# First x chunk by column halves, warm-up products on a constant, second q-k reload behind two sets of down weights

## The chip, the cores and the metric

The kernel runs on one NeuronCore of one Trainium2 chip. The metric is the device time of one execution in microseconds (us), as the median of several runs. Five engines work side by side: TensorE (PE) multiplies, with its weight loads shown apart as PEld; VectorE (DVE) and ScalarE (ACT) do elementwise work and empty the PSUM banks that PE writes; GpSimd (POOL) and SyncE (SP) here mostly issue transfers. Transfers (DMAs) between device memory and the on-chip buffer are issued by the queues of SP, ACT and POOL. Each engine runs its own list of instructions in order; semaphores tell it when an operand is ready.

## The reference

```python
def _A_ref(x, wqkv, wo):                       # local attention, 32 heads of 32
    qkv = (x @ wqkv) -> q, k, v
    idx = pos[:, None] - 2 * arange(8)[None, :]        # 8 keys, every second position back
    logits = einsum(q, k[idx]) * Dh ** -0.5            # -1e9 where idx < 0
    o = softmax(logits) @ v[idx]
    return o @ wo
def _B_ref(x, w_gate, w_up, w_down):           # gated feed-forward, 1024 -> 3584 -> 1024
    return (gelu(x @ w_gate) * (x @ w_up)) @ w_down
g = sigmoid((x * gate_w).sum(-1))
out = g * A + (1 - g) * B                      # x: 2048 x 1024, bfloat16
```

Both branches read the same x of 2048 rows and 1024 columns.

## The kernel before

**Products.** Every large product is done by a seven-product scheme on 2 x 2 blocks (a Strassen form). For the projections (`Unit`) the blocks come from 1024 rows of x (two chunks of 512 rows, `c1` and `c2`, transposed so that the 1024 columns lie on the partitions as 8 tiles of 128) and from 256 columns of a weight. A unit has the parts p1 (L11 by R11), p2 (L12 by R21), p5, p6, p73 and p4, four matmuls of 128x128 by 128x512 for each product. R11 is the first four column tiles of chunk 0 and R21 the last four; some operands (S1 to S4 of the weights, T1 to T4 of x) are sums that DVE forms. ACT copies out what p1, p2, p5, p6 and p4 leave in a bank; the end of p73 is emptied by a DVE addition (line 389). When that addition is late, PE cannot reuse the bank.

**Order.** The order on every engine is written out by hand. A loop runs over the units; in each turn it emits p1 of the unit, p73 of the one before, p5, then a slot of attention reductions (line 593) if one is due, p2 and p6, and p4 of the one before. Between these, background tasks (`bg`, `run_bg`) put DVE work into the stream by estimated costs and priorities; hooks (`at`, `at_end`) put single actions at the start or end of a turn. None of these costs is a measured time at run time: DVE's order is fixed when the program is built.

**Head.** `head()` runs two pairs of gate/up columns on the first 1024 rows: chunk 0 is loaded as four row tiles of 128 rows (256 KB each, rows of 2 KB), alternately by SP and ACT (`load_xn`, line 144). PE runs NWARM = 6 warm-up products on a region that DVE has set to zero (lines 148 to 152). Then `pe_transpose_chunk(0, ...)` transposes chunk 0 on PE in eight groups of four 128x128 tiles (line 217), row tile by row tile, each row tile's columns 0 to 511 and then 512 to 1023; DVE and ACT copy the groups out in turn (lines 223 and 221). The first products are p1 of the gate and up units. Chunk 1 is transposed by the same function with `by_k`, which takes the column half 0 of all four row tiles first. Weights of the two pairs (`load_pair`, line 168) follow x in SP's queue, the first halves in 128 KB pieces, then chunk 1 and the second halves.

**Attention and down weights.** Units 2 to 17 give q and k, units 18 to 25 give v. The last 256 rows of q and k of each half go out to memory (`q_d`, `k_d`, lines 512 and 513) and are read back at the end of turn QE = 18 by `spill_load` (lines 633 and 634), two transfers for each half, into space that held weights of the q and k units and their sums. DVE multiplies them much later (`spill`). In the next turn `tf_load` (line 854) loads the sets 4 and 5 of down weights, four transfers of 256 KB each, into the space of the third and fourth block of the q and k weights (last read by p73 and by p4 of unit 17). `t_forms` (lines 869 and 872) forms differences of these sets on DVE. All of these loads stand in SP's queue in the order in which they are emitted, and SP waits at each one until its space and its data are free. SP and ACT use eight semaphores for their transfers in turn, so a load also waits for the one eight before it.

Of the kernel before, what the change touches and what calls it, by code (L numbers as in the profile page):

```python
# [10 lines left out]
BF16 = mybir.dt.bfloat16  # L11
# [4 lines left out]
P = 128  # L16
SC = 512
# [5 lines left out]
NJ = 4  # L23
SJ = AC // NJ
NEG = -1.0e9
NWARM = 6
QG = 4

KB = 512
# [17 lines left out]
R_ST = 178  # L47
# [21 lines left out]
def kernel(  # L69
# [12 lines left out]
    nc = tc.nc  # L82
# [3 lines left out]
    x = A_x.rearrange("b s d -> (b s) d")  # L86
    o2 = out.rearrange("b s d -> (b s) d")
    KT = D // P
    HK = KT // 2
# [13 lines left out]
    def reg(kb, n):  # L103
        o = int(kb * KB)
        return arena[:, o:o + n]

    def reg3(kb, a, b):
        return reg(kb, a * b).rearrange("p (a b) -> p a b", a=a)
# [4 lines left out]
    def regf(kb, n):  # L113
        return reg(kb, 2 * n).bitcast(F32)
# [3 lines left out]
    def bank(i):  # L118
        return banks[:, i, :]
# [15 lines left out]
    V = nc.vector  # L135
    TT = V.tensor_tensor

    with tc.manual_schedule(engines={mybir.EngineType.PE, mybir.EngineType.DVE, mybir.EngineType.Activation,
                                    mybir.EngineType.SP, mybir.EngineType.Pool}):
        xn = [reg3(R_XN + 8 * i, 4, D) for i in range(2)]  # L140

        def load_xn(c):
            for j in range(4):
                (nc.scalar if c == 0 and j % 2 else nc.sync).dma_start(
                    out=xn[c % 2][:, j, :], in_=x[c * SC + j * P:c * SC + (j + 1) * P, :])

        load_xn(0)
        warm = reg(R_ST, SC)
        V.memset(warm, 0.0)
        for i in range(NWARM):  # L150
            pw = bank((2, 4, 6, 0)[i % 4])
            nc.tensor.matmul(pw, lhsT=warm[:, 0:P], rhs=warm, start=True, stop=True)
# [44 lines left out]
        def flat(a):  # L197
            return a.rearrange("p a b -> p (a b)")
# [8 lines left out]
            f = xf[s]  # L207
            TT(out=flat(f.T3), in0=flat(f.R22), in1=flat(f.R12), op=ALU.subtract)

        def pe_transpose_chunk(c, dst, slots, by_k=False):  # L210
            order = [(j, k0) for j in range(4) for k0 in range(0, KT, 4)]
            if by_k:
                order.sort(key=lambda g: g[1])
            for n_, (j, k0) in enumerate(order):
                p_ = bank(slots[n_ % len(slots)]).bitcast(BF16)[:, 0:SC].rearrange("p (a b) -> p a b", a=4)
                for kk in range(4):
                    nc.tensor.transpose(out=p_[:, kk, :], in_=xn[c % 2][:, j, (k0 + kk) * P:(k0 + kk + 1) * P],  # L217
                                        identity=ident[:])
                d = dst[:, k0:k0 + 4, j * P:(j + 1) * P]
                if n_ % 2 == 1:  # L220
                    nc.scalar.copy(out=d, in_=p_)
                else:
                    V.tensor_copy(out=d, in_=p_)
# [92 lines left out]
        def gu_forms(w, sm, m):  # L316
            r = lambda k0, a: (lambda kt: w[:, m, k0 + kt, a * P:(a + 1) * P])
            z = lambda n: (lambda kt: sm[:, n, m, kt, :])
            return {"L11": r(0, 0), "L12": r(HK, 0), "L22": r(HK, 1), "S1": z(0), "S2": z(1), "S3": z(2), "S4": z(3)}
# [7 lines left out]
        for c in range(2, 4):  # L327
            dst = (xf[1].c1, xf[1].c2)[c - 2]
# [91 lines left out]
        def bg(gen, prio, wake):  # L420
            t = Task(gen, prio, wake)
            tasks.append(t)
            tasks.sort(key=lambda t_: t_.prio)
            return t
# [41 lines left out]
        def at(n, fn):  # L466
            hooks.setdefault(n, []).append(fn)
# [4 lines left out]
        def at_end(n, fn):  # L472
            post.setdefault(n, []).append(fn)
# [7 lines left out]
        def h_task(G, U, i, s):  # L481
            h_store(G, U, i, s)
            yield 1.14 if i < NSC else 2.3
# [148 lines left out]
        def spill_load(s):  # L632
            nc.sync.dma_start(out=qb[s], in_=q_d[s][:])
            nc.sync.dma_start(out=kb[s], in_=k_d[s][:])
# [4 lines left out]
        def spill(s):  # L639
            while reduced[0] < 2 * NT:  # L640
                yield None
            accs = []
            for g, (x, y) in enumerate(SPILL[s]):
                for i, ef in enumerate((x, y)):
                    t = QG * g + 2 * i
                    if credit[0] > 1.5:
                        qk_mult2(pair_at(*ef), qb[s][:, t, :], kb[s][:, t, HALO:HALO + AC], AC, KV)
                        yield 2.21
                        continue
                    for j in range(2):  # L650
                        qk_mult(reg3(ef[j], NWIN, AC), qb[s][:, t + j, :], kb[s][:, t + j, HALO:HALO + AC])
                        yield 1.14
                if credit[0] > 1.5:
                    TT(out=pair_at(*x), in0=pair_at(*x), in1=pair_at(*y), op=ALU.add)
                    yield 2.21
                else:
                    for j in range(2):
                        TT(out=reg(x[j], NWIN * AC), in0=reg(x[j], NWIN * AC), in1=reg(y[j], NWIN * AC), op=ALU.add)
                        yield 1.14
                lo, hi = (reg3(o, NWIN, AC) for o in x)  # L660
                TT(out=lo, in0=lo, in1=hi, op=ALU.add)
                yield 1.14
                accs.append(lo)
            slotq.append(lambda: spill_reduce(s, accs))
# [132 lines left out]
                n_ = Q0 + NT * s + t  # L797
                due(n_ + 4, bg(qk_prods(units[n_], s, t), 2, n_ + 2))
        QE = Q0 + 2 * NT
        at_end(QE, lambda: (spill_load(0), spill_load(1)))  # L800
        bg(spill(0), 4, QE + 2)
        bg(spill(1), 4, QE + 2)
        pv_task = [bg(pv_all(), 4.2, QE + 3)]
# [11 lines left out]
        def r_parts(half, nh, i0=0, i1=NK):  # L815
            ns = slice(nh * SC, (nh + 1) * SC)
            if i0 < NH_:
                e = min(i1, NH_)
                yield slice(i0, e), B_w_down[:, ns].rearrange("(i two p) n -> p i two n", two=2, p=P)[:, i0:e, half, :]
            if i1 > NH_:  # L820
                a = max(i0, NH_)
                yield slice(a, i1), A_wo[:, ns].rearrange("(p t) n -> p t n", t=NT)[:, 4 * half + a - NH_:4 * half + i1 - NH_, :]
# [19 lines left out]
        N1 = 4  # L842
        TB = Q0 + 2 * NT + 1
        TC = NQKV + 1

        def tf_set(q):
            o = R_TF[q % 3] if q < N1 or q >= N1 + 2 else R_TB[q - N1]
            return [reg3(o + NP * k, NP, SC) for k in range(4)]

        def tf_load(q):  # L850
            i0 = NP * q
            for k, a in enumerate(((0, 0), (0, 1), (1, 0), (1, 1))):
                for sl, src in r_parts(*a, i0, i0 + NP):
                    nc.sync.dma_start(out=tf_set(q)[k][:, sl.start - i0:sl.stop - i0, :], in_=src)
# [23 lines left out]

        for q, b in enumerate((2, 3, 5)):
            at(Q0 + b, lambda q=q: tf_load(q))  # L880
        at(TB, lambda: [tf_load(q) for q in range(N1, N1 + 2)])
        at(TC, lambda: [tf_load(q) for q in range(N1 + 2, min(N1 + 5, NQ))])
        tft = bg(t_forms(), 6, Q0 + 4)

# [364 lines left out]
        def head():  # L1249
            xs, f = xf[0], []  # L1250
            for w, sm, o in ((raw0, sums0, R_ATTN), (raw1, sums1, R_PROD)):
                for m in range(2):
                    u = Unit(gu_forms(w, sm, m), xs, ("gate", "up")[m], None)
                    u.T = reg3(o + 4 * m, 2, SUP)
                    f.append(u)
            units[0:Q0] = f[2:]
            for u, x, v, y, z in zip(f, (3, 5, 1, 7), (1, 7, 3, 5), (0, 2, 4, 6), (1, 3, 5, 7)):
                u.lie(x, v, y, z)
            f[3].fin = lambda: bg(h_task(f[2].T, f[3].T, 1, 0), 0, now[0] + 1)
            T = lambda o_, a, b_: TT(out=flat(o_), in0=flat(a), in1=flat(b_), op=ALU.subtract)  # L1260
            s0, s1 = sums_pair(raw0, sums0), sums_pair(raw1, sums1)

            pe_transpose_chunk(0, xs.c1, (3, 5, 1, 7))
            f[0].p1_()
            f[1].p1_()
            patterns()
            f[0].p2()
            f[1].p2()
            f[2].p1_()
            f[3].p1_()  # L1270
            f[2].p2()
            pe_transpose_chunk(1, xs.c2, (3, 5, 1), True)
            T(xs.T1, xs.R12, xs.R11)
            next(s0)
            next(s1)
            f[3].p2()
            for c in range(2):
                gate_chunk(c, bank(3 + 2 * c))
            next(s0)
            T(xs.T2, xs.R22, xs.T1)  # L1280
            next(s1)
            T(xs.T3, xs.R22, xs.R12)
            for i, u in enumerate(f):
                u.p5(regf(R_XN + 2 * i, SC))
            for g in (s0, s0, s1, s1):
                next(g)
            T(xs.T4, xs.R21, xs.T2)
            for u in f:
                u.p6()
            next(sq0)  # L1290
            next(sq0)
            for u in f[:3]:
                u.p73()
            for g in (sq0, sq0, sq1, sq1):
                next(g)
            for u in f[:3]:
                u.p4()
            bg(h_task(f[0].T, f[1].T, 0, 0), 0, Q0 + 1)

        head()  # L1300
        for b in range(Q0, n):
            now[0] = b
# [55 lines left out]
```

## Time and profile before

| | |
|---|---|
| median of 3 runs | 719.1 us (717.49 to 719.21) |
| the profiled execution | 718.77 us, span 717.0 us |
| PE busy | 705.7 us (98%) |
| DVE busy | 669.0 us (93%) |
| ACT, POOL busy | 330.7 us, 142.4 us |
| chain that ended last | PE 91%, DVE 3%, DMA 3% |

The span is what the trace covers; the profiled execution's own time is 1.8 us more. The timeline gives the start of an instruction or of a row of like ones, how long it took, and in brackets how long its engine had been idle before it and what ended the idle time. The table of waits gives, for an engine and a line, what was waited for: total us, how many times, the longest. The rows of transfers give count, size and median us from issue to landing. Since PE is busy for nearly all of the span, what counts is where PE stands still and what it waits for there.

### The profile page before, as it was taken

What the parts mean: (1) busy time and instruction counts of PE and PEld (TensorE: products, weight loads), DVE (VectorE), ACT (ScalarE), POOL (GpSimd) and SP (SyncE); (2) the same over time, 40 slices, a digit from 0 to 9 for tenths busy, and PEclk for the clock granted to TensorE, in tenths of its full rate; (3) what the DMA queues carried; (4) which work ended last, traced back from release to release, by engine and by line L of the source; (5) the groups of instructions that cost most, each with busy time, mean ns of one, the idle gap of its engine ahead of it and who ended that gap; (6) DMA issues with size and microseconds to landing.
All of it is one profiled execution on the core that took longest, in us unless ns stands there. A gap on an engine that the chain in (4) does not pass through costs nothing.

```text
span 717.0 us, 10673 instructions
## 1 busy us (share of the span) xinstructions
PE 705.7 (98%) x4043; PEld 408.4 (57%) x4099; DVE 669.0 (93%) x633; ACT 330.7 (46%) x603; POOL 142.4 (20%) x245
## 2 busy tenths in 40 slices
PE   8999999999999999999999999999999999999998
PEld 5466666655544444444444444444447886758887
DVE  3969989989999999999999999999699899799997
ACT  5554445444466565555555555555322321132431
POOL 1223445323232332121300010101100002100011
PEclk9999999999999999999999999999999999999999
DMA  9975434478285667765762763474950799995951
GB/s 252 274 188 169 151 125 154 155 239 306 92 269 175 214 216 240 223 214 180 234 178 89 279 208 122 161 262 148 426 226 29 300 405 397 417 431 218 403 211 59
DMA packets 94707, 162.03 MB, mean 226 GB/s; under 512 B 23632, under 2 KB 71152, under 8 KB 90304
## 3 DMA queue, kind: packets, MB, share of 16 engines
q1 hardware_dynamic: 77632, 105.46, 42.7%
q0 software_dynamic: 16304, 48.29, 19.9%
q10 hardware_dynamic: 720, 7.60, 2.7%
q8 instruction: 32, 0.52, 0.3%
q14 instruction: 19, 0.16, 0.1%
HBM read 112.17 MB, written 54.14 MB: 232 GB/s over the span
## 4 chain that ended last, share of the span: by engine, by line
PE 91%; DVE 3%; DMA 3%; issue 1%; ACT 0%; DVEq 0%; POOLq 0%; ACTq 0%
PE banks L343 63%; PE banks L1046 19%; PE banks L1079 7%; PE banks L593 2%; DMA arena<-h_d 1%; DMA h_d<-arena 1%; DVE arena L389 1%; DVE arena L753 1%; PE banks L217 1%; DVE arena L747 1%; DMA arena<-in_A_x_dram 0%; DVE arena L313 0%; DVE arena L588 0%; DVE arena L1260 0%; DVE arena L581 0%
## 5 line engine op out<-in xcount | busy, mean ns | idle before, releaser
L343 PE MATMUL banks<-arena 128*128 128x512 bf16 x2191 | 484.1, 379 | 5.4 <-DVE arena L389 2.2
L343 PEld LDWEIGHTS <-arena 128*128 128x128 bf16 x2240 | 245.9, 110 | 242.2 <-issue 8.1
L1046 PE MATMUL banks<-arena 128*128 128x256 bf16 x1260 | 138.5, 273 | 0.0
L1046 PEld LDWEIGHTS <-arena 128*128 128x128 bf16 x1260 | 123.3, 98 | 15.4 <-issue 0.5
L389 DVE TENSOR_TENSOR arena<-banks,arena 128x1024 bf16<-128x1024 f32 x80 | 97.4, 1219 | 11.1 <-PE banks L343 6.5
L370 ACT COPY arena<-banks 128x512 f32<-128x512 f32 x80 | 46.9, 587 | 129.7 <-PE banks L343 129.7
L351 ACT CAST arena<-banks 128x512 bf16<-128x512 f32 x104 | 60.9, 585 | 42.8 <-PE banks L343 42.2
L747 DVE TENSOR_TENSOR arena<-arena 128x4096 bf16<-128x4096 bf16 (+1 forms) x41 | 73.5, 1818 | 0.3
L753 DVE TENSOR_TENSOR arena<-arena 128x2048 bf16<-128x2048 bf16 (+2 forms) x54 | 68.1, 1261 | 0.9
L250 POOL DMA_DIRECT2D h_d<-arena x28 | 20.4, 731 | 222.6 <-DVE arena L244 144.6
L1079 PE MATMUL banks<-arena 128*128 128x512 bf16 x281 | 62.6, 379 | 0.7 <-DMA arena<-h_d 0.4
L378 ACT COPY banks<-banks 128x512 f32<-128x512 f32 x80 | 45.6, 570 | 23.7 <-PE banks L343 20.8
L1004 DVE TENSOR_TENSOR arena<-arena 128x2304 bf16<-128x2304 bf16 x40 | 53.3, 1352 | 0.5
L365 ACT COPY banks<-banks 128x512 f32<-128x512 f32 x80 | 46.1, 576 | 14.2 <-PE banks L343 13.1
L1051 ACT COPY banks<-banks 128x256 f32<-128x256 f32 x60 | 21.4, 356 | 62.2 <-PE banks L1046 62.0
L588 DVE TENSOR_TENSOR arena<-arena 128x4096 bf16<-128x4096 bf16 x21 | 47.9, 2284 | 0.3 <-ACT arena L370 0.2
L1079 PEld LDWEIGHTS <-arena 128*128 128x128 bf16 x288 | 28.1, 98 | 34.2 <-DMA arena<-h_d 0.9
L349 ACT ACTIVATE arena<-banks 128x512 bf16<-128x512 f32 x56 | 33.5, 597 | 20.4 <-PE banks L343 20.4
L927 DVE TENSOR_TENSOR arena<-arena 128x2048 bf16<-128x2048 bf16 (+1 forms) x40 | 41.7, 1111 | 0.0
L313 DVE TENSOR_TENSOR arena<-arena 128x1024 bf16<-128x1024 bf16 x64 | 41.1, 685 | 0.5
L1012 DVE TENSOR_TENSOR arena<-arena 128x2304 bf16<-128x2304 bf16 x28 | 37.7, 1352 | 0.2
L244 DVE TENSOR_TENSOR arena<-arena 128x2048 bf16<-128x2048 bf16 x28 | 34.0, 1216 | 2.8 <-ACT arena L351 2.8
(92 smaller groups left out, 448.2 us busy)
## 6 DMA issues: line engine op xcount, KB each, us to landing
arena<-t_d SPq DMA_DIRECT2D x8, 2304.0 KB, 9.6
h_d<-arena POOLq DMA_DIRECT2D x28, 512.0 KB, 4.4
arena<-w_c SPq DMA_DIRECT2D x12, 1152.0 KB, 13.2
t_d<-arena POOLq DMA_DIRECT2D x36, 256.0 KB, 5.4
arena<-h_d SPq DMA_DIRECT2D x6, 1536.0 KB, 12.1
arena<-in_B_w_down_dram SPq DMA_DIRECT2D x28, 256.0 KB, 6.6
arena<-in_B_w_gate_dram SPq DMA_DIRECT2D x14, 512.0 KB, 5.4
arena<-in_B_w_up_dram SPq DMA_DIRECT2D x14, 512.0 KB, 4.2
```

The source lines that it names most:

```text
L343: self.pe = nc.tensor.matmul(ps, lhsT=self.L[form](kt), rhs=rhs[:, kt, :], start=(start and kt == 0), stop=(kt == HK - 1), skip_group_chec ...
L351: nc.scalar.copy(out=o_, in_=i_)
L365: nc.scalar.copy(out=self.Y, in_=self.X)
L370: nc.scalar.copy(out=self.p5s, in_=self.V)
L378: nc.scalar.copy(out=self.Z, in_=self.Y)
L389: TT(out=self.T[:, :, c2s], in0=pair, in1=self.p5s.rearrange("p (o n) -> p o n", o=1).to_broadcast([P, 2, SC]), op=ALU.add)
L588: TT(out=dst, in0=_win_ap(q, [[sq, 2], [0, NWIN], [1, AC]]), in1=_win_ap(k, [[sk, 2], [-DIL, NWIN], [1, AC]]), op=ALU.mult)
L747: TT(out=prod2[:, t % 4:t % 4 + m, :], in0=flat(ab).rearrange("p (o n) -> p o n", o=1).to_broadcast([P, m, NWIN * AC]), in1=_win_ap(v[:, t ...
L753: TT(out=h(0) if w > 1 else o_[:, t:t + m, :], in0=h(0), in1=h(1), op=ALU.add)
L1004: TT(out=o_, in0=a, in1=b_, op=op)
L1046: nc.tensor.matmul(c(i, h, j), lhsT=l[:, kt, j * P:(j + 1) * P], rhs=r[:, kt, :], start=False, stop=(kt == KH - 1), skip_group_check=True)
L1079: nc.tensor.matmul(ps, lhsT=L[:, i, j * P:(j + 1) * P], rhs=R[:, i, :], start=(start and q == 0), stop=(q == NK - 1), skip_group_check=not ...
```

## The change

- Chunk 0 of x is loaded by four transfers in another cut: columns 0 to 511 of the row tiles 0 and 1 (SP) and 2 and 3 (ACT), then columns 512 to 1023 likewise. Each is again 256 KB, in pieces of 1 KB. They stay ahead of all weights in SP's queue.
- Eight warm-up products read a constant of ones (one element per partition, read again and again) in place of six on a zeroed region; the zeroing on DVE is gone. The dummy activation on ACT reads the constant too.
- Chunk 0 is transposed in the order of column halves, as chunk 1 was: the argument `by_k` is gone and its order holds for both.
- The reload of q and k of the second half moves from directly behind the first half's to behind the sets 4 and 5 of down weights. In SP's queue the eight transfers of line 854 pass the two of lines 633 and 634. The instruction streams of PE, DVE, ACT and POOL are otherwise the same, instruction by instruction.

```diff
-NWARM = 6
+NWARM = 8
...
         def load_xn(c):
             for j in range(4):
-                (nc.scalar if c == 0 and j % 2 else nc.sync).dma_start(
-                    out=xn[c % 2][:, j, :], in_=x[c * SC + j * P:c * SC + (j + 1) * P, :])
-
-        load_xn(0)
-        warm = reg(R_ST, SC)
-        V.memset(warm, 0.0)
+                nc.sync.dma_start(out=xn[c % 2][:, j, :], in_=x[c * SC + j * P:c * SC + (j + 1) * P, :])
+
+        for h in range(2):
+            cs = slice(h * HK * P, (h + 1) * HK * P)
+            for i, q in enumerate((nc.sync, nc.scalar)):
+                q.dma_start(out=xn[0][:, 2 * i:2 * i + 2, cs],
+                            in_=x[2 * i * P:2 * (i + 1) * P, cs].rearrange("(j p) d -> p j d", p=P))
+        warm = nc.const_aps.tensor(1.0, [P, SC], BF16)
...
-        def pe_transpose_chunk(c, dst, slots, by_k=False):
+        def pe_transpose_chunk(c, dst, slots):
             order = [(j, k0) for j in range(4) for k0 in range(0, KT, 4)]
-            if by_k:
-                order.sort(key=lambda g: g[1])
+            order.sort(key=lambda g: g[1])
...
-        at_end(QE, lambda: (spill_load(0), spill_load(1)))
+        at_end(QE, lambda: spill_load(0))
...
-        at(TB, lambda: [tf_load(q) for q in range(N1, N1 + 2)])
+        at(TB, lambda: ([tf_load(q) for q in range(N1, N1 + 2)], spill_load(1)))
...
-            pe_transpose_chunk(1, xs.c2, (3, 5, 1), True)
+            pe_transpose_chunk(1, xs.c2, (3, 5, 1))
```

## Prediction

> **What bounds the kernel now.** I read the page first (busy times and the chain), then PE's waits, since PE is on nearly all of the chain, and then the timelines of the two places that the change touches.
>
> ```profile
> span 717.0 us, 10673 instructions
> PE 705.7 (98%) x4043; PEld 408.4 (57%) x4099; DVE 669.0 (93%) x633; ACT 330.7 (46%) x603; POOL 142.4 (20%) x245
> PE 91%; DVE 3%; DMA 3%; issue 1%; ACT 0%; DVEq 0%; POOLq 0%; ACTq 0%
> ```
>
> PE stands still for 717.0 - 705.7 = 11.3 us of the span, so no change that only takes waits away can bring more than 1.6%. Its waits for a released operand, the largest first:
>
> ```profile
> PE banks L343 <- DVE arena L389: 2.2, 2, 1.4
> PE banks L152 <- DVE arena L149: 1.2, 1, 1.2
> ```
>
> Two waits for DVE's addition at line 389 are 2.2 us, and one of them is 1.4. The wait at line 152 is for the zeroing of the warm-up region at the very start. PE and DVE around the 1.4 us:
>
> ```profile
> 163.76 1.48 PE L593 MATMUL banks<-arena,ones_r 128*32 128x512 bf16 x24
> 165.17 7.99 PE L343 MATMUL banks<-arena 128*128 128x512 bf16 x35
> 174.61 7.72 PE L343 MATMUL banks<-arena 128*128 128x512 bf16 x35 [1.44 <-DVE arena L389]
> ```
> ```profile
> 149.41 1.23 DVE L389 TENSOR_TENSOR arena<-banks,arena 128x1024 bf16<-128x1024 f32 x1 [1.42 <-PE banks L343]
> ...
> 157.46 1.22 DVE L389 TENSOR_TENSOR arena<-banks,arena 128x1024 bf16<-128x1024 f32 x1
> 159.22 1.22 DVE L869 TENSOR_TENSOR arena<-arena 128x2048 bf16<-128x2048 bf16 x1 [0.55 <-DMA arena<-in_B_w_down_dram]
> 160.48 1.42 DVE L872 TENSOR_TENSOR arena<-arena 128x1024 bf16<-128x1024 bf16 x2
> 162.82 1.23 DVE L869 TENSOR_TENSOR arena<-arena 128x2048 bf16<-128x2048 bf16 x1 [0.92 <-DMA arena<-in_B_w_down_dram]
> 164.08 1.42 DVE L872 TENSOR_TENSOR arena<-arena 128x1024 bf16<-128x1024 bf16 x2
> 165.41 1.22 DVE L389 TENSOR_TENSOR arena<-banks,arena 128x1024 bf16<-128x1024 f32 x1
> 166.55 1.75 DVE L688 TENSOR_REDUCE md<-banks 128x192 f32<-128x1536 f32 x1
> ...
> 173.34 1.22 DVE L389 TENSOR_TENSOR arena<-banks,arena 128x1024 bf16<-128x1024 f32 x1
> ```
>
> At 149.41 DVE is ahead and waits for PE. Then it waits 0.55 and 0.92 us for down weights (sets 4 and 5), runs without a gap, and is late at 173.34: PE, out of work at 165.17 + 7.99 = 173.16, goes on at 174.61. Why the down weights are late stands in SP's timeline and SP's waits:
>
> ```profile
> 139.20 0.34 SPq L634 DMA_DIRECT2D arena<-k_d  x1
> 148.18 0.33 SPq L633 DMA_DIRECT2D arena<-q_d  x1
> ...
> 149.07 5.63 SPq L854 DMA_DIRECT2D arena<-in_B_w_down_dram  x8
> ```
> ```profile
> SPq L633 <- DMA q_d<-arena: 8.0, 1, 8.0
> ```
>
> The reload of the second half's q waits 8.0 us for the last q store to land, and the eight down-weight loads stand behind it in the queue.
>
> **Step 1: the reload goes behind the down weights.** Two issues (about 0.33 us each) pass behind eight; nothing is added. The four loads of set 4 then need only p73 of unit 17 to be over, set 5 needs its p4. ACT tells when that is: its copies follow p5 of unit 18 (after that p73) and that p4.
>
> ```profile
> 144.17 0.59 ACT L370 COPY arena<-banks 128x512 f32<-128x512 f32 x1 [1.97 <-PE banks L343]
> ...
> 146.76 0.59 ACT L351 CAST arena<-banks 128x512 bf16<-128x512 f32 x1 [0.29 <-PE banks L343]
> ```
> ```profile
> DMA to landing us min/median/max: 3.4/6.6/9.2
> ```
>
> So set 4 can be issued by 144.2 and set 5 by 146.8. The second row is for all loads of line 854. At 5.63 / 8 = 0.7 us an issue, the last loads go out by 146.3 and 148.9. With the median, the sets land by about 152.9 and 155.5; with the longest, by 155.5 and 158.1. DVE asks for set 4 at 157.46 + 1.14 = 158.60 (1.14 is the distance of L389 and L688 above) and for set 5 at 158.60 + 2.59 = 161.19 (2.59: 162.82 to 165.41). Both waits go, with 3 us to spare in the worse case. DVE then reaches the second L389 at 161.19 + 2.59 = 163.78 instead of 165.41, and would start L688 at 164.92. What is late next is PE: L688 reads the reductions of line 593, which end at 163.76 + 1.48 = 165.24. So L688 starts at about 165.30, 1.25 us earlier than before; the last L389 ends 1.25 us earlier, at 173.31, and PE goes on at 173.36: PE gains 1.25 us of its 1.44. Ends of this term: 0 (another wait takes the place), 1.44 (the whole stall). The moved reload lands by about 149.6 + 9.2 = 158.8 at worst; its products stand in DVE's order behind all those of the first half, so nothing asks for it yet and I cost the delay at 0. If a reader stood at 158 us, SP's order would cost the delay in full.
>
> **Step 2: the head.** Nothing of PE's first 18 us is hidden; it is a chain.
>
> ```profile
> 1.20 2.74 PE L152 MATMUL banks<-arena 128*128 128x512 bf16 x6 [1.20 <-DVE arena L149]
> 4.12 3.12 PE L217 MATMUL banks<-ident,arena 128*128 128x128 bf16 x32 [0.19 <-DMA arena<-in_A_x_dram]
> 7.53 1.89 PE L343 MATMUL banks<-arena 128*128 128x512 bf16 x8 [0.29 <-DVE arena L223]
> ```
> ```profile
> 4.10:6.50 2.40, 2.38 (x23) 2.38 (x24) 1.00 1.12 292
> 6.55:7.05 0.50, 0.50 (x11) 0.50 (x9) 1.00 1.29 284
> ```
>
> The second fence is the transposes alone in two stretches (PE busy and count, then weight loads and count): 24 weight loads in 2.40 us are 0.10 us each, 9 in 0.50 us are 0.056. PE doubles its pace at about 6.5 us, though the granted clock reads 1.00 in both. Transfers that matter here:
>
> ```profile
> 0.74 0.91 ACTq L144 DMA_DIRECT2D arena<-in_A_x_dram  x2
> ...
> 1.67 0.43 SPq L168 DMA_DIRECT2D arena<-in_B_w_gate_dram  x1
> ```
> ```profile
> arena<-in_A_x_dram SPq DMA_DIRECT2D x1, 256.0 KB, 3.3
> ...
> arena<-in_A_x_dram ACTq DMA_DIRECT2D x1, 256.0 KB, 4.7
> arena<-in_B_w_gate_dram SPq DMA_DIRECT2D x1, 128.0 KB, 4.7
> ```
>
> - *Warm-up.* Without the zeroing PE starts at about 0.75, as ACT's first issue does, instead of 1.20. Eight products at 2.74 / 6 = 0.46 at most end by 4.4, x lands at about 4.1: PE is fed without the 0.19 us gap, and transposes start at about 4.3 (before: 4.12), a loss of 0.2 at most. No row shows an operand read again from one element; its nearest row is the 0.46 above, which I take.
> - *Smaller pieces of x.* Same bytes, same four issues. Down weights come in pieces of 1 KB and land in 3.4 us at best, x in pieces of 2 KB in 3.3: I take 0.1 to 0.3 us later, for the weights behind too. The last x before lands at about 1.2 + 4.7 = 5.9, after at about 6.1, still before PE needs it.
> - *Order.* p1 needs only the four groups of the first half. Before, the next to last group is among them and PE waits 0.29 us for its copy; after, the copies are long over and p1 follows the last transpose.
> - *Sum.* From 4.3 at 0.104 us, 21.6 transposes are done by 6.55 and the other 10.4 at 0.056 by 7.13: p1 at 7.15 instead of 7.53, 0.38 us less. Were the doubling earlier by the 0.45 us that PE starts earlier, it would be 6.94: 0.59 less. I take 0.45. Ends: 0.88 less (p1 cannot pass the gate weights, 1.67 + 4.7 + 0.3 = 6.65) and 0.3 more (late x, no doubling in time).
>
> [...]
>
> Does the gain live on? PE's next wait is for a DVE sum:
>
> ```profile
> 18.62 6.65 PE L343 MATMUL banks<-arena 128*128 128x512 bf16 x30 [0.26 <-DVE arena L313]
> ```
> ```profile
> DVE arena L389 <- PE banks L343: 4.9, 3, 2.6
> ```
>
> That sum follows the transposes of chunk 1 and so comes earlier with them. The second row (waits of DVE from 30 to 60 us) says that DVE waits 4.9 us for PE there, and at 149.41 again 1.42: PE leads, and what it gains at 7 us is still there at 174.
>
> **Sum.** 1.25 + 0.45 = 1.7 us off the profiled execution's 718.77 (span 717.0 and 1.8 around it): 717.1. That execution lies 0.3 below the median of the runs, 719.1. I say 717.0. From no change a measurement of this kernel can tell about 0.3%, 2.2 us: 716.9 against the median. My forecast lies just at that bound.
>
> **Rivals.**
> - *Early pace, full stall gone.* PE doubles its pace one step earlier. Then transposes run at 0.056 us and wait for x and gate weights: p1 at 6.65, 0.88 less; with 1.44 at 174 that is 2.3 us, 716.4. For it: PE is busy from 0.75 on without the gap. Against: 1.20 to 6.5 was long, and the gap short. [...]
> - *Only the reload.* x in 1 KB pieces comes late enough to eat the 0.45: 718.77 - 1.25 = 717.5; if 0.3 is lost besides, 717.8.
> - *The reload step moves only the wait.* DVE's 1.5 us go, but it meets PE's reductions or another landing, and PE still resumes near 174.6: only the head's 0.45 is left, 718.3. For it: L688 takes 0.4 of DVE's 1.63 at once. Against: nothing else in DVE's rows there is a wait.
> - *Slower: the constant.* If a product on a repeated element takes w instead of 0.46 us, transposes start at 0.75 + 8w. At double pace p1 comes at 0.75 + 8w + 32 x 0.056 = 2.54 + 8w. It passes 7.53 from w = 0.62 on, eats the 1.25 too from w = 0.78, and from w = 1.05 the kernel is slower by over 2.2 us: 721 or more. For it: no row of such an operand. Against: the same count of columns is streamed.
>
> **How the numbers follow.** Forecast as summed: 0.50, its own range 716.0 to 717.8, and half of it lies below 716.9. Early pace: 0.28, all below. Only the reload: 0.07. Only the head: 0.05. Slower (the constant): 0.10. So faster by over 0.3%: 0.25 + 0.28 = 0.53; within: 0.25 + 0.07 + 0.05 = 0.37; slower: 0.10. The range goes from 715.4 (1.44 + 0.88, and a microsecond for the place of the pace's step) to 719.2, which takes in all but the slow case and the far ends.
>
> **What would show it.** Step 1 is right if line 854 is issued before 149 us, DVE has no wait at line 869 and PE's wait of 1.44 us falls to about 0.2. Step 2 is right if warm-up products start near 0.75 at 0.43 to 0.46 us, the transposes follow without a gap, and the first p1 starts between 6.7 and 7.2. The prediction is wrong if PE waits at line 217 for x, if warm-up products outlast 4.5 us, or if another wait for line 389 opens after 174.

## The result and the profile after

| | before | after |
|---|---|---|
| median of 15 runs each, taken side by side | 718.23 us (717.49 to 720.34) | 717.04 us (716.74 to 718.48) |
| ratio | | 0.9982 (95% interval 0.9974 to 0.9990) |
| the profiled execution | 718.77 us, span 717.0 | 717.04 us, span 715.3 |

The change takes 1.2 us off the median; the ratio says 0.18% (1.3 us), with an interval that leaves out "no change". The time is the forecast one (717.0); the way to it is only half the forecast one. The page of the changed kernel begins:

```profile
span 715.3 us, 10731 instructions
PE 709.2 (99%) x4101; PEld 408.3 (57%) x4101; DVE 668.7 (93%) x632; ACT 330.7 (46%) x603; POOL 141.9 (20%) x245
```

PE is at work for all but 6.1 us of the span, where it was 11.3 (before's records lack some 60 matmuls, so part of this difference is counting). PE's largest waits in the changed kernel (total us, times, longest), of which the first is the start of the program; line numbers are one or two higher than before, and line 390 is the addition that was line 389:

```profile
PE banks L154 <- PEq L1343: 0.8, 1, 0.8
PE banks L344 <- DVE arena L390: 0.7, 2, 0.5
PE banks L218 <- DMA arena<-in_A_x_dram: 0.3, 1, 0.3
PE banks L344 <- DVE arena L314: 0.3, 1, 0.3
PE banks L218 <- ACT arena L350: 0.2, 1, 0.2
PE banks L344 <- DMA arena<-in_B_w_up_dram: 0.2, 1, 0.2
```

The waits for line 390 were 2.2 us, 1.4 at most. In their place stands nothing large. In the head the waits for the zeroing (1.2 us) and for a copy ahead of p1 (0.29) are gone; the wait for x has grown from 0.19 to 0.29, and one of 0.20 for up weights is new. PE and then DVE at the place of the old 1.44 us:

```profile
163.98 1.48 PE L594 MATMUL banks<-arena,ones_r 128*32 128x512 bf16 x24
165.39 7.99 PE L344 MATMUL banks<-arena 128*128 128x512 bf16 x36
173.59 8.58 PE L344 MATMUL banks<-arena 128*128 128x512 bf16 x39 [0.20 <-DVE arena L390]
```
```profile
157.69 1.22 DVE L390 TENSOR_TENSOR arena<-banks,arena 128x1024 bf16<-128x1024 f32 x1
158.82 1.22 DVE L870 TENSOR_TENSOR arena<-arena 128x2048 bf16<-128x2048 bf16 x1
160.07 1.42 DVE L873 TENSOR_TENSOR arena<-arena 128x1024 bf16<-128x1024 bf16 x2
161.40 1.22 DVE L870 TENSOR_TENSOR arena<-arena 128x2048 bf16<-128x2048 bf16 x1
...
163.99 1.22 DVE L390 TENSOR_TENSOR arena<-banks,arena 128x1024 bf16<-128x1024 f32 x1
165.52 1.76 DVE L689 TENSOR_REDUCE md<-banks 128x192 f32<-128x1536 f32 x1 [0.31 <-PE banks L594]
...
172.32 1.22 DVE L390 TENSOR_TENSOR arena<-banks,arena 128x1024 bf16<-128x1024 f32 x1
```

DVE no longer waits at line 870, reaches line 390 early at 163.99, stands 0.31 us for the reductions at line 689, and does the last addition at 172.32 instead of 173.34. SP's queue shows why:

```profile
142.02 6.22 SPq L855 DMA_DIRECT2D arena<-in_B_w_down_dram  x8
148.47 0.34 SPq L634 DMA_DIRECT2D arena<-q_d  x1
149.71 0.34 SPq L635 DMA_DIRECT2D arena<-k_d  x1
```

The down weights go out 7 us earlier, and the reload comes behind them. The head, PE's first 9 us:

```profile
0.78 3.57 PE L154 MATMUL banks<-const-bfloat16-1.0 128*128 128x512 bf16 x8 [0.78 <-PEq L1343]
4.64 2.89 PE L218 MATMUL banks<-ident,arena 128*128 128x128 bf16 x32 [0.29 <-DMA arena<-in_A_x_dram]
7.37 1.03 PE L344 MATMUL banks<-arena 128*128 128x512 bf16 x4
8.60 1.04 PE L344 MATMUL banks<-arena 128*128 128x512 bf16 x4 [0.20 <-DMA arena<-in_B_w_up_dram]
```

The warm-up starts 0.42 us earlier and its eight products end at 4.35, but x is not there before 4.64. p1 starts 0.16 us earlier than the 7.53 of before, and the second p1 (up) waits for its weights. PE's wait at 18.84, for the same DVE sum as the wait at 18.62 before, is where the head's balance can be read:

```profile
18.84 2.98 PE L344 MATMUL banks<-arena 128*128 128x512 bf16 x13 [0.26 <-DVE arena L314]
```

So the head costs 0.22 us in this pair of executions.

**Where the 1.7 us between the two spans are.** The head costs 0.22 us, and the stall at 174 is 1.44 - 0.20 = 1.24 us shorter. The rest comes after 500 us, at two places that the edits do not name. Before, PE waits near 527 us for the load of h_d, and its last row of line 1046 takes a little longer than the same row after (line 1047):

```profile
527.04 17.44 PE L1079 MATMUL banks<-arena 128*128 128x512 bf16 x78 [0.36 <-DMA arena<-h_d]
644.32 69.27 PE L1046 MATMUL banks<-arena 128*128 128x256 bf16 x630
```
```profile
642.76 69.09 PE L1047 MATMUL banks<-arena 128*128 128x256 bf16 x630
```

The last rows start 1.56 us apart and the stall at 174 ends 1.02 us apart (174.61 and 173.59), so 0.54 us go to the wait for h_d, which the second execution of the kernel before does not have. The last row itself is 69.27 - 69.09 = 0.18 us shorter. That difference is no matter of the execution: PE and ACT lose 0.17 to 0.19 us near 650 us in all seven profiled executions of kernels that load x in whole rows, and in none of the seven with x in column halves. Why the first load should matter there is open. Together -0.22 + 1.24 + 0.54 + 0.18 = 1.74. PE's wait for line 389 near 279 us reads 0.75 before and 0.54 after, but its end lies 104.89 us behind the end of the stall at 174 in both: nothing was lost there, and the 0.21 us more of idle time fit one matmul whose record is missing before (the rows have 1055 and 1076).

### The profile page after: what moved, and what is told of

The parts are those of the page before. It is cut to its first block, busy times and chain, and to the rows that moved or that the text cites. A ratio compares the mean times of both kernels' runs of the same rounds, so it can differ in the third digit from the quotient of the medians.

```text
span 715.3 us, 10731 instructions
## 1 busy us (share of the span) xinstructions
PE 709.2 (99%) x4101; PEld 408.3 (57%) x4101; DVE 668.7 (93%) x632; ACT 330.7 (46%) x603; POOL 141.9 (20%) x245
## 4 chain that ended last, share of the span: by engine, by line
PE 94%; DVE 3%; DMA 1%; issue 1%; SPq 0%; ACT 0%; DVEq 0%
PE banks L344 64%; PE banks L1047 19%; PE banks L1080 9%; PE banks L594 2%; DMA arena<-in_B_w_up_dram 1%; DVE arena L390 1%; DVE arena L754 1%; DVE arena L748 1%; DVE arena L314 0%; DVE arena L1261 0%; DVE arena L582 0%; DVE arena L245 0%; PE banks L218 0%; SPq L149 0%; PE banks L273 0%
```

## The experiments

Theory at the outset: the gain is the reload's, and the head gives nothing because x in smaller pieces lands later. Rival: the head does bring its 0.45 us, and the profiled execution hides it. The first four kernels ran side by side with the kernel before (718.24 us, median of 33 runs), the next three likewise (718.33, 29 runs); the rest are single profiled executions.

**The moved reload alone, with the old head.**

```diff
-        at_end(QE, lambda: (spill_load(0), spill_load(1)))
+        at_end(QE, lambda: spill_load(0))
...
-        at(TB, lambda: [tf_load(q) for q in range(N1, N1 + 2)])
+        at(TB, lambda: ([tf_load(q) for q in range(N1, N1 + 2)], spill_load(1)))
```

> The kernel before with the moved reload alone. Theory A (the reload brings what the whole change brings, the new head brings nothing or costs a little): DVE has no wait at line 854's data (lines 869), PE's wait of 1.44 us near 174 falls to about 0.2, the time is 1.25 us under the kernel before, as much as with the whole change or up to 0.2 us better. Theory B (the prediction's sum: reload 1.25, head 0.45): 1.25 us under before, 0.45 us above the whole change. Theory C (the gain of the whole change comes from elsewhere, such as the end of the kernel): less than 0.5 us under before.

Measured: 717.48 us (716.75 to 719.53), ratio 0.9988 (0.9977 to 0.9999). DVE's lag against before falls by 1.25 us between 157 and 166 us and the stall is 0.20, as in the changed kernel. So at 174 us this part does in full what the forecast said, without the head; by the medians it brings 0.76 us. Yet the profiled execution took 719.42 us, more than before's; its loss is in the head:

```profile
1.20 2.74 PE L152 MATMUL banks<-arena 128*128 128x512 bf16 x6 [1.20 <-DVE arena L149]
4.80 3.60 PE L217 MATMUL banks<-ident,arena 128*128 128x128 bf16 x32 [0.86 <-DMA arena<-in_A_x_dram]
8.48 1.62 PE L343 MATMUL banks<-arena 128*128 128x512 bf16 x4
```

x landed late here (4.8 instead of 4.1), PE stood 0.86 us, and its pace doubled only at 9.71 us instead of 6.58. p1 came at 8.48, and PE's wait of 18.62 stands at 20.16: 1.54 us lost.

**The head alone, with the reload where it was.**

```diff
-        at_end(QE, lambda: spill_load(0))
+        at_end(QE, lambda: (spill_load(0), spill_load(1)))
...
-        at(TB, lambda: ([tf_load(q) for q in range(N1, N1 + 2)], spill_load(1)))
+        at(TB, lambda: [tf_load(q) for q in range(N1, N1 + 2)])
```

> The changed kernel with the reload put back where it was: only the head's edits stay (x by column halves in 1 KB pieces, eight warm-up products on the constant, transposes by column halves). Theory A: x lands 0.5 to 0.9 us later, p1 starts near 7.4 us but the up product's p1 waits for its weights, the second wait at 18.6 us comes 0.2 us later than before; PE's wait near 174 is about 1.4 us as before; time equal to before within 0.3 us. Theory B: 0.45 us under before.

Measured: 718.74 us (717.40 to 719.37), ratio 0.9996 (0.9985 to 1.0008): no gain from the head by itself. p1 starts at 7.33, as theory A had it, and PE's wait of 18.62 stands at 18.58, not 0.2 us later. Two things in its profile were not expected. DVE's waits (0 to 31 us first, then from 145 to 180):

```profile
DVE arena L314 <- DMA arena<-in_B_w_up_dram: 1.6, 1, 1.6
```
```profile
DVE arena L390 <- PE banks L344: 1.4, 1, 1.4
DVE arena L870 <- DMA arena<-in_B_w_down_dram: 0.7, 1, 0.7
```

The second half of the up weights came 1.6 us late near 20 us; against the changed kernel this execution is 1.2 us later from there on. And DVE waits for only one set of down weights, for 0.7 us; PE's stall is 0.59, not 1.44, though the reload stands in front of the sets as before.

**x in whole rows again, the rest of the change kept**, with the transposes by column halves as in the change, and with them row by row as before (there `by_k` is put back as well).

```diff
-        for h in range(2):
-            cs = slice(h * HK * P, (h + 1) * HK * P)
-            for i, q in enumerate((nc.sync, nc.scalar)):
-                q.dma_start(out=xn[0][:, 2 * i:2 * i + 2, cs],
-                            in_=x[2 * i * P:2 * (i + 1) * P, cs].rearrange("(j p) d -> p j d", p=P))
+        for j in range(4):
+            (nc.scalar if j % 2 else nc.sync).dma_start(out=xn[0][:, j, :], in_=x[j * P:(j + 1) * P, :])
```

> The changed kernel, with chunk 0 of x loaded as before by row tiles in 2 KB pieces; transposes by column halves, warm-up constant and moved reload stay. Theory A (the 1 KB pieces are what delays x and the weights behind it): x lands at 4.1 to 5.9 us as before, the gate weights at about 6.4 and the up weights at about 6.8, p1 starts between 6.9 and 7.3 us, the chain reaches PE's wait near 18.6 us about 0.3 to 0.5 us earlier than before, and the time is 1.5 to 1.8 us under before. Rival (the delay came from the order of issues or from the earlier warm-up products, not from the pieces): weights land at about 7.3 and 8.5 us again and the time is that of the whole change.

Measured: 717.03 us (716.77 to 718.07), ratio 0.9980 (0.9972 to 0.9989).

> As the one with row tiles in 2 KB pieces, but chunk 0 is transposed row tile by row tile as before: of the head's edits only the warm-up products on the constant stay, beside the moved reload. Theory A: landings as before, p1 starts with the last row tile's copy at about 7.1 to 7.5 us, 0.1 to 0.4 us before the kernel before (the earlier start of the warm-up products can bring the doubling of PE's pace forward); time 1.25 to 1.6 us under before. Rival (transposing by halves brings nothing): the same time as with transposes by halves on row tiles.

Measured: 716.98 us (716.62 to 717.83), ratio 0.9978 (0.9968 to 0.9987). Both equal the changed kernel within their intervals. The cut of x by column halves and the order of the transposes bring nothing; with whole rows and the old order p1 starts at 7.52 and PE's wait stands at 18.61, where the changed kernel has 7.37 and 18.84. So the column halves start p1 0.15 us earlier and reach PE's wait near 18.8 us 0.23 later: what p1 gains, the up weights behind x, which hold the second p1 back, take again and more.

Neither expectation for the landings is borne out as a whole. With whole rows the first gate and up weights do land sooner than with column halves (5.1 and 5.0 us after their issue against 5.5 and 6.3), as theory A had it, but p1 starts at 7.62, because PE waits 0.33 and 0.50 us for x, and the time is that of the whole change, as the rival had it. That profiled execution took 718.07 us, the most of its twelve; DVE waits 1.5 us near 20 us for the second half of the up weights in it, as in the head alone.

The kernel with whole rows and the old order differs from the moved reload alone in one thing, the warm-up: eight products on the constant for six on a zeroed region. It took 716.98 against 717.48 us, and none of its 9 runs lay above 718 us, where 4 of 12 did. The two intervals overlap (0.9968 to 0.9987 and 0.9977 to 0.9999), so these runs favour the longer and earlier warm-up without settling it.

**Fewer and more warm-up products.** Four in the changed kernel, and ten with x in whole rows (transposes by column halves).

```diff
-NWARM = 8
+NWARM = 4
```

> The changed kernel with four warm-up products instead of eight: they end at about 2.5 us, and PE is idle for about 2 us until x lands. Theory A (a gap between warm-up and transposes lets PE's doubling of pace slip to a later step, and the changed head's use is that it closes this gap): the step to double pace comes after 8 us, the transposes all run at 0.107 us, p1 starts at 8.1 us or later and its products run at 0.43 us for a while; 1.0 to 2.5 us slower than the changed kernel, so about as slow as the kernel before or slower. Theory B (what counts is only when x and the weights land): p1 at about 7.4 to 7.7 us and the time of the changed kernel within 0.3 us.

Measured: 717.83 us (717.16 to 718.95), ratio 0.9994 (0.9985 to 1.0003): 0.8 us over the changed kernel's median, most of the gain gone, though the two intervals overlap. Its profiled execution was its fastest run; PE there:

```profile
0.78 1.86 PE L154 MATMUL banks<-const-bfloat16-1.0 128*128 128x512 bf16 x4 [0.78 <-PEq L1343]
4.54 3.34 PE L218 MATMUL banks<-ident,arena 128*128 128x128 bf16 x32 [1.89 <-DMA arena<-in_A_x_dram]
7.71 1.96 PE L344 MATMUL banks<-arena 128*128 128x512 bf16 x8
```

With the gap of 1.89 us the step in pace lies at 7.31 and p1 starts at 7.71, as theory B had it (7.4 to 7.7) and not theory A (8.1 or later). In this execution the end of the head did not suffer (18.87 against 18.84); where the 0.8 us of the median lies, which is more than theory B allows, one execution does not show.

> Chunk 0 by row tiles in 2 KB pieces, transposed by halves, moved reload, and ten warm-up products on the constant: they end at about 5.0 us, so no gap is left for x landing at up to 5.0. Theory A: the step to double pace comes between 3.9 and 7.6 us in every execution, p1 between 7.0 and 7.7; median as with eight products (717.0) or up to 0.3 us better, and fewer executions above 718. Theory B (warm-up does not matter): the two more products push the transposes back by up to 0.4 us and the time is up to 0.4 us above that of eight.

Measured: 717.17 us (716.91 to 718.26), ratio 0.9982 (0.9974 to 0.9990): the same as eight. In the profiled execution the step in pace lies at 4.92 and PE still waits 0.70 us for x, with p1 at 7.80: the products fill the gap before x but can't bring x.

**The reload between the two sets.**

```diff
-        at(TB, lambda: ([tf_load(q) for q in range(N1, N1 + 2)], spill_load(1)))
+        at(TB, lambda: (tf_load(N1), spill_load(1), tf_load(N1 + 1)))
```

> The changed kernel with the second q-k reload between the two sets of down weights: set 4 passes the reload, set 5 stays behind it. Theory A (a set is late only if it is issued after the wait for the q store and behind a second megabyte; DVE asks for set 5 at 161.2 us): set 5 is issued at 149 to 151 us and lands by 158 to 160, DVE waits at neither set, the stall at 174 is about 0.2 us as in the changed kernel, and the time is the same within 0.3 us. Theory B (every load behind that wait is late): DVE waits 0.5 to 1.5 us for set 5, PE's stall is 0.7 to 1.4 us, and 0.5 to 1.2 us of the gain is lost.

Measured: 718.06 us (716.84 to 718.76), ratio 0.9992 (0.9983 to 1.0001), 1 us over the changed kernel, though in its profile (717.60 us) DVE waits at neither set and PE's stall is 0.20. Two more profiled executions were to show where the time goes in those above 717.5:

> Second look at the kernel with the reload between the sets, whose runs lay 1 us above the changed kernel though its first profile showed the full gain of step 1. Theory A (set 5 is sometimes late): in an execution of 718 us or more DVE waits 0.5 us or more at the second line 870 and PE's stall near 174 is 0.5 to 1.4. Theory B (step 1 holds in all executions, the loss is elsewhere): the stall near 174 is 0.2 whatever the time, and the difference to 717.0 is found before 20 us (p1 later than 7.4, a wait for up weights near 20) or at the load of h_d near 527 us, 0.4 to 1.5 us together.

> Third look at the same kernel, since its executions are of two kinds (near 716.9 and 717.5 to 718.8). Theory A: in a slow one a stall near 174 of 0.5 to 1.4 us; theory B: 0.2 there, and 0.4 to 1.5 us before 20 us or at 527 us.

They took 716.96 and 717.02 us, as little as the changed kernel, with a stall of 0.20 (both on another chip than the twelve). So in three profiled executions out of three, being ahead of one set is enough for step 1, and no late set 5 was seen. The 0.6 us between 717.60 and 716.96 lie where theory B put them. In the execution of 717.60 DVE waits 0.79 us at line 314 near 19 us for the second half of the up weights, and PE, at the same point at 18.79 and 18.81, is 0.31 us later at 61.53 against 61.22; another 0.3 comes near 527 us, where weight loads on PE wait 0.6 us for h_d, against 0.2. Nothing is lost at 174. Whether the executions of 718 us and more lose theirs in the same two places is not shown: none above 717.6 was profiled. The third execution shows something else, PE in the head:

```profile
4.23 1.07 PE L218 MATMUL banks<-ident,arena 128*128 128x128 bf16 x16 [0.18 <-DMA arena<-in_A_x_dram]
6.41 1.07 PE L218 MATMUL banks<-ident,arena 128*128 128x128 bf16 x16 [1.11 <-DMA arena<-in_A_x_dram]
7.38 1.04 PE L344 MATMUL banks<-arena 128*128 128x512 bf16 x4
```

Here the pace had doubled at 3.60 us, before the first transpose: 16 of them take 1.07 us. That is the rival "early pace", and it gains nothing: PE then waits 1.11 us for the second column half of x, and p1 starts at 7.38, as in the execution with a step at 6.29.

**The parts and the kernel before, profiled a second time**, since 0.59 against 1.44 said that the stall depends on more than the reload's place.

> Second look at the head alone. Theory A (the stall near 174 varies with the landings of sets 4 and 5): 0.59 in the first look, anything from 0.5 to 1.4 now, and up weights near 20 us not late, so a time of 717.4 to 718.3. Theory B (what is common to its slow executions is the late second half of the up weights): DVE again waits 1.4 us or more at line 314 and the time is 718.5 or more.

> Second look at the reload alone. Theory A (the old head sometimes misses a step of PE's pace): if x lands by 4.3 us as in the kernel before, transposes follow the warm-up within 0.3 us, the pace doubles near 6.5, p1 is near 7.5 and the time 716.8 to 717.3; if x lands near 4.75, the gap is 0.6 to 0.9, p1 7.6 to 8.5 and the time 717.6 to 719.5. Theory B (the head does not decide): p1 near 7.5 with a time above 717.8, or 8.4 with a time below 717.3. In both the stall near 174 is 0.2.

> Second look at the kernel before, unchanged, since two looks at the head alone (reload where it was) showed stalls of 0.59 and 0.43 us near 174 and no wait for set 4, where the first look at the kernel before had 1.44 with waits of 0.55 and 0.92. Theory A (1.44 was one of the larger cases: what the reload costs hangs on when sets 4 and 5 land in that execution): no or a short wait at the first line 869, 0.4 to 0.8 at the second, a stall near 174 of 0.4 to 0.8, and a time of 717.5 to 718.3, unless x lands late. Theory B (the old head goes with the long stall): both waits again, 0.4 or more each, and a stall of 1.2 or more.

The head alone took 717.34 us, with no late up weights, a wait of 0.54 at line 870 and a stall of 0.43. The reload alone took 717.21, with x at 4.5, a gap of 0.63, the step at 6.60 and p1 at 7.77: between the two cases that its expectation named, and below the 717.6 of the second. The kernel before took 717.97 and shows both its waits again (DVE, then PE):

```profile
158.97 1.23 DVE L869 TENSOR_TENSOR arena<-arena 128x2048 bf16<-128x2048 bf16 x1 [0.45 <-DMA arena<-in_B_w_down_dram]
...
162.58 1.23 DVE L869 TENSOR_TENSOR arena<-arena 128x2048 bf16<-128x2048 bf16 x1 [0.93 <-DMA arena<-in_B_w_down_dram]
```
```profile
174.37 1.89 PE L343 MATMUL banks<-arena 128*128 128x512 bf16 x8 [1.36 <-DVE arena L389]
```

So the stall is 1.44 and 1.36 with the old head and the reload in front, 0.59 and 0.43 with the new head and the reload in front, and 0.20 in all ten profiled executions with the reload behind set 4. The eight loads go out in the same 5.2 to 5.6 us, but land sooner with the new head. From 148.5 us on, first in the second execution of the kernel before, then in that of the head alone:

```profile
arena<-in_B_w_down_dram SPq DMA_DIRECT2D x8, 256.0 KB, 8.3
```
```profile
arena<-in_B_w_down_dram SPq DMA_DIRECT2D x8, 256.0 KB, 7.2
```

The median landing is 8.3 us in both executions with the old head, 7.6 and 7.2 with the new one. Why four transfers at 1 us should speed up eight at 150 us was not found. One thing goes with it: the next load of gate weights (512 KB) is issued 5.9 and 5.6 us after the first of the eight with the old head, 6.7 and 6.5 with the new one, so it joins them earlier where they land later. Whether that is a cause or a consequence is not shown, and since the second execution of the kernel before and the two of the head alone ran on three different chips, a difference between chips is not ruled out either.

## Why the prediction was right, and where it was wrong

**Step 1 held in its causes.** Line 855 is issued from 142.02 us, DVE waits at no set, PE's stall is 0.20, and what is late next is what was named: the reductions, which hold line 689 back by 0.31 us. The gain at that place is 1.24 us against 1.25 forecast. The landings were taken too late (set 4 by 152.9 to 155.5; it has landed by 148): the first of them was issued 2 us before the copy of ACT that I took for its signal, and the two sets took 3.5 and 4.0 us at the median, not 6.6. This lay on the safe side. The moved reload costs nothing, as said: no wait for it shows after 150 us. What step 1 took for granted is that 1.44 is the stall whatever the head does; in the two profiled executions with the new head and the reload in front it is 0.59 and 0.43, so there the move has only 0.2 to 0.4 us to win.

**Step 2 failed, in the term "smaller pieces of x".** By the prediction's own signs it is wrong: PE waits 0.29 us for x at what was line 217, and p1 at 7.37 lies outside 6.7 to 7.2. I took 0.1 to 0.3 us, "for the weights behind too", and let the last x land at 6.1, "still before PE needs it". The second transfers of x and the first gate and up weights (median us from issue to landing), in the kernel before:

```profile
arena<-in_A_x_dram ACTq DMA_DIRECT2D x1, 256.0 KB, 4.7
arena<-in_B_w_gate_dram SPq DMA_DIRECT2D x1, 128.0 KB, 4.7
arena<-in_B_w_up_dram SPq DMA_DIRECT2D x1, 128.0 KB, 4.6
```

and in the changed one:

```profile
arena<-in_A_x_dram ACTq DMA_DIRECT2D x1, 256.0 KB, 5.5
arena<-in_B_w_gate_dram SPq DMA_DIRECT2D x1, 128.0 KB, 5.5
arena<-in_B_w_up_dram SPq DMA_DIRECT2D x1, 128.0 KB, 6.3
```

That is 0.8, 0.8 and 1.7 us more. In the three other executions of the old head the second x transfer of ACT takes 4.4 to 5.2 us, the gate weights 4.8 to 5.2 and the up weights 5.1 to 5.3, so against those the cut comes to 0.3 to 1.1 us for x, 0.3 to 0.7 for gate weights and 1.0 to 1.2 for up weights. The last x lands at 6.3 (SP) and 6.7 (ACT), and since PE transposes both column halves ahead of p1, p1 hangs on it: in six executions of the changed head with eight products p1 is at 7.33 to 7.52, whether the pace doubled at 3.60 or at 6.78. So p1 at 7.15 could not be had, and the second p1 waits for the up weights besides. Over 1.7 to 4.5 us the rate is 263 to 306 GB/s in the seven profiled executions with x in 2 KB pieces and 223 to 236 in the seven with 1 KB pieces; the kernel before and the changed one:

```profile
1.70:4.50 2.80, 2.61 (x10) 0.88 (x9) 0.00 (x0) 1.46 (x2) 1.41 (x2) 1.00 0.90 306
```
```profile
1.70:4.50 2.80, 2.65 (x7) 0.63 (x5) 0.00 (x0) 1.49 (x2) 1.40 (x2) 1.00 0.74 225
```

(The last columns are the granted clock, the DMA share and GB/s.) My 0.1 to 0.3 us rested on two best landings (3.3 and 3.4 us), of which one was not at the start of the program.

**The other terms of step 2.** The warm-up without zeroing starts at 0.78 (0.75 said), and a product on the repeated element takes 0.43 us: the slower rival, which needs 0.62 or more, is out. The wait for a copy before p1 (0.29) is gone, as said.

**The sum and the rivals.** 1.25 + 0.45 was said, 1.7 us lie between the two spans; but the head costs 0.22 us there, and 0.72 come from the wait for h_d and the 0.18 us near 650, which no term names. That the forecast time came out to 0.1 us is luck: the sum was taken off one execution of 718.77 us, and the median of the kernel before in 15 runs is 718.23. Off that, the same 1.7 us would have given 716.5, and 717.04 was measured; the start was 0.5 us too high and the sum 0.5 us too good. The gain by the medians, 1.2 us, is the size of step 1 alone, which the second rival ("only the reload", 717.5, chance 0.07) described; the reload alone gave 717.48. "Early pace" (0.28) had much too large a chance: its 0.88 us had the gate weights as their only bound and forgot x itself. The measured gain, 0.18%, lies below the 0.3% that I took for the least that can be told from no change: that outcome, "within", had 0.37 against 0.53 for "faster". The lean to "faster" came from a head too good by 0.45 to 0.7 us and an early pace that can't be used. The microsecond that the range allows for the place of the pace's step was an estimate that no run shows; the step itself moved from 3.60 to 9.71 us over 14 profiled executions.

**What remains open.** The parts do not add up by medians: 0.8 us for the reload with the old head, 1.7 with the new one (718.74 to 717.04), while the stalls at 174 say the reverse (1.2 and 0.2 to 0.4). By the ratios the gap is not clear of the noise: the two parts come to 0.9988 x 0.9996 = 0.9984, within the interval of the whole change. Of the executions that were profiled, those above 717.5 us lose their time to landings that vary: x at the start (the reload alone, 1.54 us), the second half of the up weights near 20 us (the head alone, 1.2; whole rows by halves, 1.0; the reload between the sets, 0.3), h_d near 527 us (0.3 to 0.9), and, with the reload in front, sets 4 and 5. Eleven of the twelve runs of the head alone lie above 718 us, against 3 of 15 of the changed kernel, which has the same head. Why was not settled.

## What to carry to other kernels

Look in a queue's timeline for a load that waits for a store: all that is issued behind it waits too (8.0 us in the kernel before), and putting independent loads ahead of it cost nothing here (and saved 1.2 us at one stall with the old head). When a transfer at the start is cut anew, price the transfers behind it as well, and ask which landing, not which engine, sets the first product. A sum taken against one profiled execution carries that execution's luck: over four executions of the old head PE's first transpose moves from 4.12 to 4.80 us with the landing of x, and the doubling of its pace from 4.66 to 9.71. Nor is every difference in idle time a loss: where two traces hold different numbers of matmuls for the same stretch, compare the starts of the rows behind it.

## What the runs showed of the hardware that was not expected

**The step in PE's pace and the idle time before it.** The spacing of weight loads halves (24 in 2.40 us, then 9 in 0.50 us, in the kernel before) at a point that the trace's clock record marks, though the granted-clock column reads 1.00 on both sides. Over 14 profiled executions it lay at 3.60, 3.88, 4.66, 4.92, 5.35, 5.97 (twice), 6.01, 6.29, 6.58, 6.60, 6.78, 7.31 and 9.71 us. The idle time ahead of the transposes does not order them: the step came at 9.71 after 0.86 us (the reload alone), at 6.60 after 0.63 (its second execution), at 7.31 after 1.89 (four products) and at 4.92 after 0.70 (ten). By kernel, it came at 6.78 or before in the nine executions with eight or ten products on the constant, and at 4.66, 6.58, 6.60 and 9.71 with the old head. So an earlier and longer warm-up bought no earlier p1 (7.52 with whole rows and the old order, 7.53 before). That it keeps the step from coming late, where the old head, with x late, had 9.71 and lost 1.54 us, is my estimate from these executions. What sets the place of the step is not shown, nor, by a run of its own, that x late by 0.7 us is enough for the 1.54 us.

**A repeated element streamed as fast as a stored operand.** Eight products on a constant of one element per partition took 3.57 us, 0.43 us from one to the next, as products on the zeroed region did (0.43). Both are at PE's pace before it doubles (at 6.29 us with the constant, at 6.58 in the kernel before).
